# A gated linear recurrence fused with a feed-forward network: copies of v as a maximum, one exponential for the decays of a unit, copies shared out anew

## The chip, the cores and the metric

The kernel runs on one core of a Trainium2 chip. The core has a matrix engine (TensorE, PE in the profile; PEld are its weight loads), a vector engine (VectorE, DVE), a scalar engine (ScalarE, ACT), a general engine (GpSimd, POOL) and a queue engine (SyncE, SP) that here only issues DMA transfers. Each engine takes its own instructions in order; they wait for each other by semaphores. TensorE writes to PSUM, eight banks of 128 x 512 floats; all else that is on the chip lies in SBUF. The metric is the device time of one execution in microseconds (us).

## The reference

The inputs q, k, v and f_logit have the shape (4 batches, 8 heads, 768 tokens, 48), the three weights are 384 x 1536, 384 x 1536 and 1536 x 384, all in float32.

```python
f = 1.0 / (1.0 + np.exp(-f_logit))
state = np.zeros((B, H, D, D), dtype=np.float32)
for t in range(S):
    state = f[:, :, t, :, None] * state + np.einsum('bhd,bhe->bhde', k[:, :, t], v[:, :, t])
    y[:, :, t] = np.einsum('bhd,bhde->bhe', q[:, :, t], state)
...
x = np.ascontiguousarray(attn_out.transpose(0, 2, 1, 3)).reshape(B * S, H * D)
gate = np.maximum(x @ w_gate, 0.0)
val = x @ w_val
return (gate * val @ w_out).astype(np.float32)
```

So a linear attention whose state decays, channel by channel, by a factor of the token; its output, 3072 tokens by 384 channels, goes through a feed-forward network with a ReLU gate.

## The kernel before

**Tiling.** Tokens are taken in windows of 128; two windows in a row of one batch are a unit, so there are 24 windows and 12 units. `seq` goes through the four batches before it takes the next two windows of each. Four windows (two units) are a group of 512 tokens for the feed-forward part: 6 groups.

**A unit, step by step.** f, k, q and v of the unit are loaded by four DMAs of 384 KB (`load`, L533), into four buffers each. The two tokens of a pair lie beside each other in a partition, so everything comes as an even and an odd half. ScalarE makes exp(-f) in place (L609) and log(1 + that) in bf16 (`bneg`, L611). TensorE forms the cumulative sums with triangular matrices (`cum`, L618 and L619), the even ones either by two more matmuls or, where `even` is DVE, on VectorE by a subtraction (L622). ScalarE takes the exponentials of the sums with both signs (L630, L633, L640), into PSUM (`kps`, `qps`) or into SBUF (`expo`). VectorE or GpSimd multiplies them with q and k to `hats` (L652, L658). In units 0 to 5 TensorE transposes these (L692) and ScalarE or VectorE copies the result to `qkT` (L470, L471); in later units a DMA transposes (L714). TensorE forms the scores (L728); they are masked to `ptm`, by VectorE straight from PSUM (L741), or by a ScalarE copy (L736) and a GpSimd multiplication (L738). v is copied in bf16 to `vpad`, four half copies a unit, and in units 0 to 5 two more to `vrest` (`copy_on`, L470 and L471). The decays of a unit's two windows come from the totals of `bneg`: eight small matmuls against `halves` (`total`, L750) give them for both halves of the partitions, and ScalarE takes two exponentials of 64 partitions x 8 (L757), which leave the entries off the diagonal blocks of `dec` at the zeros it was filled with. The state's new part comes from TensorE (`state`, L767 or L777), the sum with the old state from VectorE (L584, or L579 for a first window), the multiplication by the decay from GpSimd (L587). The window's output comes from scores and state, transposed as the feed-forward part wants it (`intra`, L809, for windows in `pe_x`; ScalarE copies it to `xT`, L829) or in natural form (`natural`, L816 and L820; copy L834 to `xn`, and a DMA transposition, L836).

**The feed-forward part.** For each group and each of 12 blocks j of hidden columns: three matmuls for the gate and three for the value (L854), a ReLU on ScalarE (L860), the gated product on VectorE (L864) to `gT`. The first four j of group 0 are done in two halves of 256 tokens. Then 12 matmuls for each window's output (L880), a copy to `osb` on ScalarE (L895) and a store (L902). The outputs of a group are spread among the hidden products of the next one.

**What sets the order.** All operations are listed with their reads, writes, an assumed length, a latency and a priority (`Plan.add`). `Plan.schedule` goes through an assumed time and gives each engine the operation that could start first, by priority where several could; PSUM banks are given out in that run under a limit for each use (four for the feed-forward part). The order so found is written out engine by engine with the semaphore waits it needs. `chain` keeps operations of a sort in line. `first` is the order of the first loads, with what each waits for behind an @; a load also waits for the one six before it. The weights are loaded in four parts each on GpSimd's queue (L549). A table `on` names, for each unit, the engine of each step that has a choice: v00 to v11 and r0, r1 for copies of v, m00 to m11 for masks (POOL means ScalarE and GpSimd), q and k products, tq and tk for transposed copies; `q_lined` are the later units whose q products are made by token half, as the k products are. Until the planned time 24 matmuls on zeros (L939) are put ahead of TensorE's waits, as many as the planned gap takes.

Of the kernel before, what the change touches and what calls it, by code (L numbers as in the profile page):

```python
# [352 lines left out]
def bass_hgrn2_outer__then__ffn_reglu_kernel(  # L353
# [19 lines left out]
    GC = 4  # L373
# [51 lines left out]
    halves = sb("halves", [128, 2], BF16)  # L425
# [7 lines left out]
    pl.EASY = 30  # L433
# [34 lines left out]
    def copy_on(e, out, src):  # L468
        if e == "ACT":
            return sc.activation(out, src, AF.Copy)  # L470
        return engine[e].tensor_copy(out, src)  # L471

# [3 lines left out]
    def copy_t(e, n):  # L476
        return dict(occ=0.52, lat=0.16) if e == "ACT" else dict(occ=0.36, lat=0.13) if e == "DVE" else dict(occ=0.55, lat=0.1)
# [26 lines left out]
    for i in range(NA):  # L504
        fill("DVE", f"dec{i}", dec_all[:, i], 0.0, 8, -14)
# [21 lines left out]
    def load(n, u, after=()):  # L527
# [4 lines left out]
        behind = list(after) + (sent[-6:][:1] if len(sent) >= 6 else [])  # L532
# [39 lines left out]
    def new_state(kv, u, y, P):  # L572
# [4 lines left out]
        dk = [f"dec{ai}", f"dec{ai}_0", f"dec{ai}_1"]  # L577
# [12 lines left out]
    blocks = [(p, i) for p in range(NP) for i in range(3)]  # L590

    def unit(u):
# [11 lines left out]
        on.update({0: {'kps': True, 'qps': True, 'q0': 'POOL', 'q1': 'DVE', 'even': 'PE', 'm00': 'DVE', 'm01': 'DVE', 'm10': 'DVE', 'tk': 'DVE', 'm11': 'DVE', 'r1': 'ACT', 'tq': 'ACT', 'v11': 'ACT', 'v10': 'DVE', 'r0': 'DVE', 'v01': 'DVE', 'v00': 'POOL'}, 1: {'kps': True, 'r0': 'ACT', 'm01': 'DVE', 'm00': 'DVE', 'tq': 'ACT', 'v11': 'POOL', 'even': 'PE', 'tk': 'ACT', 'q1': 'DVE', 'v00': 'ACT', 'm11': 'POOL', 'r1': 'ACT', 'm10': 'DVE', 'v01': 'ACT', 'v10': 'POOL', 'q0': 'POOL', 'qps': False}, 2: {'tk': 'DVE', 'v01': 'POOL', 'kps': False, 'r1': 'ACT', 'r0': 'ACT', 'even': 'PE', 'q0': 'POOL', 'v00': 'ACT', 'v10': 'ACT', 'm00': 'DVE', 'v11': 'DVE', 'm01': 'DVE', 'm11': 'DVE', 'tq': 'DVE', 'q1': 'DVE', 'm10': 'POOL', 'qps': True}, 4: {'v10': 'ACT', 'v01': 'ACT', 'm00': 'DVE', 'q11': 'DVE', 'q00': 'POOL', 'q01': 'POOL', 'q0': 'POOL', 'kps': False, 'even': 'DVE', 'm01': 'DVE', 'v00': 'DVE', 'm10': 'POOL', 'q10': 'POOL', 'q1': 'DVE', 'm11': 'POOL', 'v11': 'DVE', 'qps': True, 'tq': 'DVE', 'r0': 'POOL', 'tk': 'DVE', 'r1': 'POOL'}, 10: {'m00': 'POOL', 'm10': 'POOL', 'q0': 'POOL', 'kps': False, 'q10': 'DVE', 'm01': 'POOL', 'q11': 'DVE', 'q00': 'POOL', 'v11': 'ACT', 'even': 'DVE', 'v01': 'DVE', 'v00': 'POOL', 'q01': 'POOL', 'q1': 'POOL', 'm11': 'DVE', 'v10': 'DVE'}, 9: {'v11': 'DVE', 'v10': 'ACT', 'even': 'DVE', 'kps': False, 'q1': 'DVE', 'm10': 'DVE', 'v00': 'ACT', 'm11': 'POOL', 'q11': 'DVE', 'm00': 'DVE', 'q00': 'DVE', 'q10': 'POOL', 'q0': 'POOL', 'q01': 'DVE'}, 3: {'kps': True, 'm00': 'POOL', 'm11': 'DVE', 'v11': 'ACT', 'm10': 'POOL', 'tk': 'ACT', 'v01': 'DVE', 'r1': 'ACT', 'tq': 'ACT', 'q1': 'POOL', 'v00': 'DVE', 'v10': 'ACT', 'q0': 'DVE', 'r0': 'POOL', 'm01': 'DVE', 'even': 'DVE', 'qps': False}, 5: {'q1': 'DVE', 'm00': 'DVE', 'kps': False, 'q11': 'POOL', 'v10': 'ACT', 'v00': 'ACT', 'even': 'DVE', 'q01': 'DVE', 'm11': 'POOL', 'q00': 'DVE', 'q0': 'POOL', 'v11': 'POOL', 'm01': 'DVE', 'q10': 'DVE', 'v01': 'DVE', 'm10': 'DVE', 'tq': 'DVE', 'r0': 'POOL', 'tk': 'ACT', 'r1': 'ACT', 'qps': False}, 11: {'q0': 'POOL', 'v01': 'ACT', 'q10': 'DVE', 'm00': 'POOL', 'q01': 'POOL', 'm11': 'POOL', 'q1': 'DVE', 'q00': 'DVE', 'kps': True, 'v11': 'ACT', 'm01': 'DVE', 'q11': 'DVE', 'even': 'PE', 'v00': 'ACT', 'm10': 'POOL', 'v10': 'POOL'}, 7: {'v10': 'POOL', 'kps': False, 'q1': 'POOL', 'v01': 'ACT', 'q11': 'POOL', 'm00': 'DVE', 'v11': 'DVE', 'even': 'PE', 'm10': 'POOL', 'm11': 'DVE', 'm01': 'DVE', 'q10': 'POOL', 'qps': False, 'q01': 'POOL'}, 8: {'m10': 'DVE', 'v11': 'ACT', 'q01': 'DVE', 'm01': 'POOL', 'even': 'DVE', 'q0': 'POOL', 'v10': 'ACT', 'q1': 'DVE', 'm00': 'DVE', 'kps': False, 'q11': 'DVE', 'q00': 'DVE', 'qps': False}, 6: {'v10': 'POOL', 'v01': 'DVE', 'q10': 'DVE', 'm10': 'DVE', 'kps': False, 'q1': 'POOL', 'even': 'PE', 'q01': 'DVE', 'm00': 'POOL', 'm01': 'POOL', 'q11': 'DVE', 'q00': 'POOL', 'm11': 'DVE', 'qps': True}}.get(u, {}))  # L604
# [64 lines left out]
        for y in range(2):  # L669
            vi = vis[y]  # L670
            for i in range(2):
# [75 lines left out]
        def total():  # L747
            for p in range(NP):
                for i in range(2):
                    mm = te.matmul(tot.ap[:, 2 * p:2 * p + 2], bn[:, i, 2 * p:2 * p + 2, :].rearrange("p h d -> p (h d)"),  # L750
                                   halves[:, :], start=(i == 0), stop=(i == 1), skip_group_check=True)
            return mm
        add("PE", total, ["halves"] + bkeys, [tot], occ=0.18, lat=PE_L, prio=P + 2, opens=[tot])
        for j in range(2):
            lo = 64 * j
            a0 = 2 * u % NA
            add("ACT", lambda lo=lo, j=j: sc.activation(  # L757
                dec_all[lo:lo + 64, a0:a0 + 2, :, j].rearrange("p b n -> p n b"),
# [148 lines left out]
    for g in range(NW // GC):  # L907
        for x in range(GC // 2):
# [3 lines left out]
            for op in pl.ops[before:]:  # L912
                op.slack = 2.5 if op.flow is not None else 0
# [112 lines left out]
```

## Time and profile before

| | us |
|---|---|
| median of 3 runs | 198.11 (197.93 to 198.9) |
| the profiled execution | 197.88 |
| its span, first to last instruction | 195.8 |
| TensorE busy | 187.1 (96%) |
| ScalarE busy | 137.9 (70%) |
| VectorE busy | 125.7 (64%) |
| GpSimd busy | 66.7 (34%) |

An engine's busy time is the time in which one of its instructions runs; matmuls overlap in the pipeline, so that the start of the next tells more of a matmul's cost than its own length. A group of instructions is named by line, engine, operation, output and inputs; behind the bar stand its busy time, the mean ns of one, and the idle time ahead of them with what ended it. The chain is followed back from the last instruction, at each step to what released it.

### The profile page before, as it was taken

What the parts mean: (1) busy time and instruction counts of PE and PEld (TensorE: products, weight loads), DVE (VectorE), ACT (ScalarE), POOL (GpSimd) and SP (SyncE); (2) the same over time, 40 slices, a digit from 0 to 9 for tenths busy, and PEclk for the clock granted to TensorE, in tenths of its full rate; (3) what the DMA queues carried; (4) which work ended last, traced back from release to release, by engine and by line L of the source; (5) the groups of instructions that cost most, each with busy time, mean ns of one, the idle gap of its engine ahead of it and who ended that gap; (6) DMA issues with size and microseconds to landing.
All of it is one profiled execution on the core that took longest, in us unless ns stands there. A gap on an engine that the chain in (4) does not pass through costs nothing.

```text
span 195.8 us, 4628 instructions
## 1 busy us (share of the span) xinstructions
PE 187.1 (96%) x1829; PEld 104.1 (53%) x1855; DVE 125.7 (64%) x227; ACT 137.9 (70%) x277; POOL 66.7 (34%) x94
## 2 busy tenths in 40 slices
PE   7899899998999999999999999999999999999995
PEld 2366585454565465555655455555555455544564
DVE  4576768948299899798997894975834423442300
ACT  4999857897699999999997775747643743344322
POOL 5179325516305835274606411603620600000000
DMA  5999999999999779999999107134544100111113
GB/s 159 324 323 198 203 254 239 203 258 257 255 301 295 211 193 308 222 236 298 161 214 173 66 20 142 44 75 112 31 106 94 44 32 8 44 40 40 40 40 121
DMA packets 74037, 31.25 MB, mean 160 GB/s; under 512 B 66209, under 2 KB 74017, under 8 KB 74017
## 3 DMA queue, kind: packets, MB, share of 16 engines
q1 hardware_dynamic: 69216, 27.43, 57.5%
q0 software_dynamic: 4800, 3.54, 11.9%
q8 instruction: 14, 0.23, 0.5%
q14 instruction: 7, 0.05, 0.1%
HBM read 25.95 MB, written 4.72 MB: 157 GB/s over the span
## 4 chain that ended last, share of the span: by engine, by line
PE 79%; ACT 14%; DVE 3%; DMA 2%; issue 1%
PE ps L854 44%; PE ps L880 22%; PE ps L809 3%; ACT qkT L470 2%; PE ps L728 2%; DMA f_in<-in_f_logit_dram 2%; ACT relu L860 2%; PE ps L692 1%; DVE ptm L741 1%; ACT vrest L470 1%; DVE vpad L471 1%; ACT vpad L470 1%; ACT ps L640 1%; ACT bneg L611 1%; ACT f_in L609 1%
## 5 line engine op out<-in xcount | busy, mean ns | idle before, releaser
L864 DVE TENSOR_TENSOR gT<-relu,ps 128x512 bf16<-128x512 bf16 (+1 forms) x76 | 49.6, 657 | 40.3 <-PE ps L854 33.7
L854 PE MATMUL ps<-xT,wv 128*128 128x512 bf16 (+1 forms) x221 | 57.8, 368 | 0.8 <-issue 0.5
L860 ACT ACTIVATE relu<-ps 128x512 bf16<-128x512 f32 (+1 forms) x76 | 43.6, 575 | 20.8 <-PE ps L854 20.4
L854 PE MATMUL ps<-xT,wg 128*128 128x512 bf16 (+1 forms) x212 | 55.6, 367 | 1.2 <-issue 0.3
L880 PE MATMUL ps<-wo,gT 128*128 128x384 bf16 (+2 forms) x300 | 52.0, 320 | 0.0
L880 PEld LDWEIGHTS ps<-wo,gT 128*128 128x128 bf16 x300 | 27.7, 98 | 19.1
L854 PEld LDWEIGHTS ps<-xT,wv 128*128 128x128 bf16 x228 | 21.1, 97 | 22.0
L854 PEld LDWEIGHTS ps<-xT,wg 128*128 128x128 bf16 x228 | 20.8, 97 | 18.9
L738 POOL TENSOR_TENSOR ptm<-ptm,seen 128x512 bf16<-128x512 bf16 x18 | 20.5, 1153 | 27.6 <-ACT ptm L736 27.5
L895 ACT ACTIVATE osb<-ps 128x384 f32<-128x384 f32 (+2 forms) x25 | 11.9, 481 | 21.7 <-PE ps L880 21.7
L587 POOL TENSOR_TENSOR st<-ssum,dec 128x384 bf16<-128x384 f32 x16 | 13.5, 846 | 27.7 <-DVE ssum L584 26.8
L741 DVE TENSOR_TENSOR ptm<-ps,seen 128x512 bf16<-128x512 f32 x30 | 19.0, 683 | 1.9 <-PE ps L728 1.6
L658 DVE TENSOR_TENSOR hats<-k_in,expo 64x384 bf16<-64x384 f32 x20 | 14.1, 706 | 0.3
L829 ACT ACTIVATE xT<-ps 128x384 bf16<-128x384 f32 x17 | 10.3, 605 | 3.7 <-PE ps L809 3.5
L736 ACT ACTIVATE ptm<-ps 128x512 bf16<-128x512 f32 x18 | 10.2, 601 | 3.6 <-PE ps L728 3.6
L470 ACT ACTIVATE vpad<-v_in 64x384 bf16<-64x384 f32 x23 | 12.0, 520 | 0.4
L658 POOL TENSOR_TENSOR hats<-q_in,expo 64x384 bf16<-64x384 f32 x7 | 7.2, 1022 | 12.6 <-ACT expo L633 12.3
L609 ACT ACTIVATE f_in<-f_in 128x768 f32<-128x768 f32 x12 | 10.1, 842 | 1.1 <-DMA f_in<-in_f_logit_dram 1.0
L939 PE MATMUL ps<-zeros 128*128 128x512 bf16 x35 | 9.8, 423 | 1.1 <-ACT dec L757 0.9
L611 ACT ACTIVATE bneg<-f_in 128x768 bf16<-128x768 f32 x12 | 10.0, 837 | 0.2
L471 POOL CAST vpad<-v_in 64x384 bf16<-64x384 f32 x12 | 6.4, 533 | 10.0 <-DMA v_in<-in_v_dram 6.5
L584 DVE TENSOR_TENSOR ssum<-ps,st 128x384 f32<-128x384 f32 x16 | 8.8, 551 | 1.1 <-PE ps L767 1.0
(79 smaller groups left out, 195.3 us busy)
## 6 DMA issues: line engine op xcount, KB each, us to landing
f_in<-in_f_logit_dram SPq DMA_DIRECT2D x12, 384.0 KB, 4.9
v_in<-in_v_dram SPq DMA_DIRECT2D x12, 384.0 KB, 5.2
q_in<-in_q_dram SPq DMA_DIRECT2D x12, 384.0 KB, 4.9
k_in<-in_k_dram SPq DMA_DIRECT2D x12, 384.0 KB, 4.9
out_dram<-osb SPq DMA_DIRECT2D x16, 192.0 KB, 2.7
out_dram<-osb SPq DMA_DIRECT2D x14, 96.0 KB, 2.2
wg<-in_moe_w_gate_dram POOLq DMA_DIRECT2D x4, 288.0 KB, 6.4
wv<-in_moe_w_val_dram POOLq DMA_DIRECT2D x4, 288.0 KB, 7.6
```

Source lines behind the costliest of these rows:

```text
L470: return sc.activation(out, src, AF.Copy)
L587: add(e, lambda: engine[e].tensor_tensor(t4(s_new), t4(tmp), rate, ALU.mult), [key] + dk, [f"S{b}_{y}"], prio=P + 2, **(dict(occ=0.79, lat ...
L609: add("ACT", lambda cut=cut: sc.activation(raw["f"][:, cut], raw["f"][:, cut], AF.Exp, scale=-1.0), [f"f{li}"], [f"f{li}"], prio=P, **act_ ...
L611: add("ACT", lambda: sc.activation(bn[:, :, :, 0:D], by_i["f"], AF.Ln, bias=1.0), [f"f{li}", f"bneg{bi}"], [f"bn{bi}"], prio=P, **act_t(2 ...
L658: op = add(e, lambda i=i, n=n, x=x, e=e, y=y, lo=lo, exps=exps: engine[e].tensor_tensor(hats[64 * i:64 * i + 64, hi, y, x, :, 0:D], by_i[n ...
L738: add("POOL", lambda pt=pt, mask=mask: gp.tensor_tensor(pt, pt, mask, ALU.mult), [f"raw{mis[y]}_{j}", "seen"], [f"raw{mis[y]}_{j}", f"ptm{ ...
L741: add("DVE", lambda pt=pt, mask=mask, s=sj[j]: ve.tensor_tensor(pt, s.ap[:, :].rearrange("p (n t) -> p n t", n=NP), mask, ALU.mult), [sj[j ...
L854: mm = te.matmul(bank.ap[:, 0:n], wt[:, kt, j * 128:(j + 1) * 128], xT[xi][:, kt, n0:n1], start=(kt == 0), stop=(kt == NK - 1))
L860: add("ACT", lambda: sc.activation(relu[ri][:, 0:n], gate.ap[:, 0:n], AF.Relu), [gate], [f"relu{ri}"], prio=P, **act_t(n))
L864: add("DVE", lambda: ve.tensor_tensor(gT[gi][:, j, n0:n1], relu[ri][:, 0:n], val.ap[:, 0:n], ALU.mult), [val, f"relu{ri}"], [f"gT{gi}_{j}_ ...
L880: mm = te.matmul(bank.ap[:, 0:cut[1] - cut[0]], gT[gi][:, j, r * C:(r + 1) * C], wo[:, j, cut[0]:cut[1]], start=(j == 0), stop=(j == NJ - 1))
L895: add("ACT", lambda bank=bank, oi=oi, cut=cut, wide=wide: sc.activation(osb[oi][:, cut[0]:cut[1]], bank.ap[:, 0:wide], AF.Copy), [bank], [ ...
```

## The change

- A copy of v can go to a third place, `DVE1`: VectorE takes a maximum over an added axis of length one (`tensor_reduce`) in place of a copy. 15 of the 60 half copies of v (`vpad` and `vrest`) are of this form; plain VectorE copies fall from 14 to 3.
- `halves` gets a second half of columns, and a 16-column matmul ahead of the totals (`other` against `away`) adds 8 x 2 x 16 = 256 wherever the entry is to be zero, so that one exponential of 128 partitions x 16 gives all decays of a unit and `dec` is no longer filled.
- Copies of outputs (`o0`, `o1`) and of x (`x0`, `x1`) have an engine by unit: 15 of 25 output copies and 7 of 24 x copies stand on VectorE.
- In every unit the k exponential now stays in PSUM (`kps` true), where VectorE's product reads it; the q products that VectorE made from `expo` in SBUF move to GpSimd or to factors in PSUM (`qps`).
- The order: another `first`; five loads in flight instead of six; a lower priority of the feed-forward part on TensorE (60 for 20); a smaller margin on DMA landings in the plan (1 for 2.5, from the planned time 34 for 30); five j of group 0 in halves instead of four; `pace` holds the cumulative sums of units 4 to 11 behind given products; other `pe_x` and `q_lined`. `longer` is empty, since `0 - size` is never positive.

The lines, cut; of the table `on` the entries that differ are given by unit as before>after:

```diff
-    first = 'f0 f1 v0 q0 k0 v1 f2 wg0@f2 wg2@f0 wv0@k0 wg1@f2 wv1@f0 wv3@f0 k1 q1 k2 wv2@k2 q2@wv1 wg3@q2 wo0@f0 wo2@f1 wo1@f1 wo3@k0 f3 k3@wv2 q3 v2 v3@wo2'.split()
+    first = 'f0 v0 f1 k0 q0 f2 wg2@f2 wg0@f2 wv0@f0 wv1@v0 k1 wg1@k1 q1 wv2@q1 v1 k2@wv0 q2 wg3@q2 wv3@v0 wo1@f0 wo0@f1 wo2@f0 wo3@f0 f3@wg2 q3@wv0 k3@wg1 v2@wo1 v3@wv0'.split()
-    pe_x = {0, 1, 2, 3, 4, 5, 6, 7, 8, 10, 11, 14, 15, 16, 17, 22, 23}
-    q_lined = {0, 1, 3, 4, 5, 6, 7, 9, 10}
+    pe_x = {0, 1, 2, 3, 4, 5, 6, 7, 9, 10, 11, 12, 13, 21, 22, 23}
+    q_lined = {0, 1, 4, 7, 8, 9, 10}
...
-    pl.EASY = 30
+    pl.EASY = 34
...
     def copy_on(e, out, src):
+        if e == "DVE1":
+            return ve.tensor_reduce(out, src.unsqueeze(len(src.shape)), mybir.AxisListType.X, ALU.max)
...
     def copy_t(e, n):
+        if e == "DVE1":
+            return dict(occ=0.47, lat=0.13)
...
-        behind = list(after) + (sent[-6:][:1] if len(sent) >= 6 else [])
+        behind = list(after) + (sent[-5:][:1] if len(sent) >= 5 else [])
...
         def total():
+            te.matmul(tot.ap[:, 0:4 * NP], other[:, :], away[:].rearrange("p n b j -> p (n b j)"), start=True, stop=False,
+                      skip_group_check=True)
             for p in range(NP):
                 for i in range(2):
-                    mm = te.matmul(tot.ap[:, 2 * p:2 * p + 2], bn[:, i, 2 * p:2 * p + 2, :].rearrange("p h d -> p (h d)"),
-                                   halves[:, :], start=(i == 0), stop=(i == 1), skip_group_check=True)
+                    mm = te.matmul(tot.ap[:, 4 * p:4 * p + 4], bn[:, i, 2 * p:2 * p + 2, :].rearrange("p h d -> p (h d)"),
+                                   halves[:].rearrange("p b j -> p (b j)"), start=False, stop=(i == 1), skip_group_check=True)
...
-        for j in range(2):
-            lo = 64 * j
-            a0 = 2 * u % NA
-            add("ACT", lambda lo=lo, j=j: sc.activation(
-                dec_all[lo:lo + 64, a0:a0 + 2, :, j].rearrange("p b n -> p n b"),
-                tot.ap[lo:lo + 64, 0:2 * NP].rearrange("p (n b) -> p n b", n=NP), AF.Exp, scale=-1.0),
...
+        add("ACT", lambda: sc.activation(dec_all[:, a0:a0 + 2, :, :].rearrange("p b n j -> p n b j"),
+                                         tot.ap[:, 0:4 * NP].rearrange("p (n b j) -> p n b j", n=NP, b=2), AF.Exp, scale=-1.0),
+            [tot], [f"dec{a0}", f"dec{a0 + 1}"], prio=P + 3, occ=0.2, lat=0.12)
...
-            add("ACT", lambda: sc.activation(lined, bank.ap[:, 0:HD].rearrange("q (n i t) -> q n i t", n=NK, i=2), AF.Copy),
+            add(e, lambda: copy_on(e, lined, bank.ap[:, 0:HD].rearrange("q (n i t) -> q n i t", n=NK, i=2)),
                 [bank], x_key, prio=P + 8, occ=0.48, lat=0.16)
...
-              prio=P + 20, opens=[gate])
+              prio=P + 60, opens=[gate])
...
-                add("ACT", lambda bank=bank, oi=oi, cut=cut, wide=wide: sc.activation(osb[oi][:, cut[0]:cut[1]], bank.ap[:, 0:wide], AF.Copy),
-                    [bank], [f"osb{oi}_{n}"], prio=P, **act_t(wide))
+                add(e, lambda bank=bank, oi=oi, cut=cut, wide=wide, e=e: copy_on(e, osb[oi][:, cut[0]:cut[1]], bank.ap[:, 0:wide]),
+                    [bank], [f"osb{oi}_{n}"], prio=P, **(act_t(wide) if e == "ACT" else dve_t(wide)))
...
-                op.slack = 2.5 if op.flow is not None else 0
-        for r0, r1, js in {0: [(0, 2, range(0, 4)), (2, 4, range(0, 4)), (0, 4, range(4, 12))]}.get(g, [(0, GC, range(NJ))]):
+                op.slack = 1 if op.flow is not None else 0
+        for r0, r1, js in {0: [(0, 2, range(0, 5)), (2, 4, range(0, 5)), (0, 4, range(5, 12))]}.get(g, [(0, GC, range(NJ))]):
...
+    pace = {4: 0, 6: 22, 9: 29, 8: 32, 10: 46, 5: 6, 7: 18, 11: 44}
+    for u, n in pace.items():
+        firsts[u].follows.append(inner[n])
```

```text
unit 0: m01 DVE>POOL, q1 DVE>POOL, r0 DVE>POOL, v00 POOL>DVE, v01 DVE>POOL, v10 DVE>DVE1, v11 ACT>DVE, x0 o0 o1 ACT>DVE
unit 1: m10 DVE>POOL, m11 POOL>DVE, qps False>True, r1 ACT>DVE1, tk ACT>DVE, v11 POOL>DVE, x0 o0 o1 ACT>DVE
unit 2: even PE>DVE, kps False>True, qps True>False, q1 DVE>POOL, r1 ACT>DVE1, tk tq DVE>ACT, v11 DVE>DVE1, x0 x1 o0 o1 ACT>DVE
unit 3: even DVE>PE, m01 m11 DVE>POOL, qps False>True, tk ACT>DVE, v00 DVE>DVE1, v01 DVE>POOL, x0 o0 o1 ACT>DVE
unit 4: kps False>True, v00 DVE>DVE1, v11 DVE>POOL, x0 o0 o1 ACT>DVE
unit 5: even DVE>PE, kps False>True, m00 DVE>POOL, m11 POOL>DVE, q1 DVE>POOL, r0 POOL>DVE1, r1 ACT>POOL, v01 DVE>ACT, v11 POOL>DVE1
unit 6: kps False>True, m10 DVE>POOL, v01 DVE>DVE1, v10 POOL>DVE1, o0 o1 ACT>DVE
unit 7: even PE>DVE, kps False>True, v11 DVE>DVE1, x1 o1 ACT>DVE
unit 8: kps False>True, q00 q01 q11 DVE>POOL, o0 ACT>DVE
unit 9: kps False>True, q00 q01 q11 DVE>POOL, v00 ACT>DVE1, v10 ACT>POOL, v11 DVE>DVE1
unit 10: kps False>True, qps False>True, m10 POOL>DVE, v01 v10 DVE>DVE1, o0 ACT>DVE
unit 11: even PE>DVE, m10 POOL>DVE, q00 q10 q11 DVE>POOL, v00 v11 ACT>POOL
```

More of the change, by code (lines that the diff above doesn't have):

```diff
@@ L424, in bass_hgrn2_outer__then__ffn_reglu_kernel @@
     below = sb("below", [128, C], BF16)
-    halves = sb("halves", [128, 2], BF16)
+    halves = sb("halves", [128, 2, 2], BF16)
+    other = sb("other", [128, 128], BF16)
+    away = sb("away", [128, NP, 2, 2], BF16)
     seen = sb("seen", [128, C], BF16)
@@ L836, in out_of @@
+            add(e, lambda: copy_on(e, xn[ni][:, :], bank.ap[:, 0:HD]), [bank], [f"xn{ni}"], prio=P + 8,
+                **(act_t(HD) if e == "ACT" else dve_t(HD)))
             op = add("SP", lambda: sy.dma_start(dst, xn[ni][:, :], transpose=True),
@@ L954, in bass_hgrn2_outer__then__ffn_reglu_kernel @@
     stores = [op for op in order["SP"] if op.writes and op.writes[0].startswith("out")]
+    size = len(order["DVE"]) + sum(max(0, len(waits[op]) - 1) for op in order["DVE"])
+    longer = set(order["DVE"][-80:][:max(0, 0 - size)])
+    spare = sb("spare", [128, 1], BF16)
     def run(name, eng):
```

43 lines of the change are left out of this document (26 added, 17 removed).

## The prediction

> **What bounds the kernel now.** I read the page first, then busy time by stage, the chain that ended last, TensorE's instructions in time, and the duration groups.
>
> ```profile
> span 195.8 us, 4628 instructions
> ...
> PE 79%; ACT 14%; DVE 3%; DMA 2%; issue 1%
> ```
>
> The chain's shares put TensorE first; the 14% on ScalarE lie almost wholly in the front. By stage (start and end, length; then busy us and instructions of TensorE, its weight loads, VectorE, ScalarE, GpSimd; granted clock, DMA share, GB/s):
>
> ```profile
> 6.04:21.85 15.81, 14.17 (x204) 8.61 (x208) 11.54 (x22) 15.55 (x34) 10.48 (x14) 1.00 1.23 268
> 21.85:54.20 32.35, 31.42 (x387) 19.19 (x390) 21.82 (x40) 24.68 (x50) 12.77 (x16) 1.00 1.11 242
> 54.20:185.60 131.40, 129.65 (x1169) 69.64 (x1188) 89.61 (x147) 92.17 (x186) 40.81 (x45) 1.00 0.57 131
> ```
>
> The clock is granted in full. In the first of these stages ScalarE is busy 15.55 of 15.81 us, and TensorE's 14.17 contain matmuls on zeros that compute nothing. From 21.85 on TensorE hardly rests. The chain in order of time (start, us, what), and TensorE's own instructions around the points that matter:
>
> ```profile
> 0.81 3.44 DMA f_in<-in_f_logit_dram
> 4.26 0.85 ACT f_in L609
> ...
> 21.16 0.19 ACT dec L757
> ...
> 51.07 0.51 PE ps L809 x28
> ...
> 66.46 0.17 PE ps L816 x4
> 66.63 0.20 PE ps L820 x8
> ...
> 69.71 0.45 PE ps L777 x16
> ...
> 71.56 0.55 PE ps L728 x16
> ...
> 165.51 3.88 PE ps L854 x18
> ...
> 181.07 1.95 PE ps L880 x12
> ```
>
> ```profile
> 6.70 0.34 PE L750 MATMUL ps<-halves,bneg 128*128 128x2 bf16 x8
> 6.90 3.18 PE L939 MATMUL ps<-zeros 128*128 128x512 bf16 x14
> ...
> 18.99 0.49 PE L854 MATMUL ps<-xT,wg 128*128 128x256 bf16 x3
> ...
> 21.85 0.49 PE L854 MATMUL ps<-xT,wv 128*128 128x256 bf16 x3
> 22.18 0.49 PE L854 MATMUL ps<-xT,wg 128*128 128x256 bf16 x3
> 22.51 0.49 PE L854 MATMUL ps<-xT,wv 128*128 128x256 bf16 x3
> ...
> 23.27 0.50 PE L854 MATMUL ps<-xT,wg 128*128 128x256 bf16 x3
> ...
> 48.54 0.41 PE L809 MATMUL ps<-ptm,vpad 128*32 128x128 bf16 x16 [0.57 <-DVE vpad L471]
> ```
>
> From 4.26 to 21.35 the chain is ScalarE's queue. After it, one matmul of 512 columns costs 3.88/18 = 0.216 us, one of 384 columns 1.95/12 = 0.163, three of 256 columns 22.18 - 21.85 = 0.33, and the one stop of size is 0.57 us at 48 us (idle time and its releaser in brackets). So the time is the front up to steady hidden products, plus a fixed amount of matmul, plus stops. The change can win at most what the front wastes and that stop; it loses wherever it lets TensorE wait later.
>
> **The change part by part.** Prices, from the groups (out of the last part of each line: busy us, mean ns) and single rows:
>
> ```profile
> L609 ACT ACTIVATE f_in<-f_in 128x768 f32<-128x768 f32 x12 | 10.1, 842 | 1.1 <-DMA f_in<-in_f_logit_dram 1.0
> L630 ACT ACTIVATE ps<-ps 128x384 f32<-128x384 f32 x8 | 3.7, 478 | 0.0
> L470 ACT ACTIVATE qkT<-ps 128x1024 bf16<-128x1024 bf16 x6 | 5.9, 1017 | 0.0
> L757 ACT ACTIVATE dec<-ps 64x8 f32<-64x8 f32 x24 | 4.3, 180 | 0.9 <-PE ps L750 0.6
> L829 ACT ACTIVATE xT<-ps 128x384 bf16<-128x384 f32 x17 | 10.3, 605 | 3.7 <-PE ps L809 3.5
> L652 DVE TENSOR_TENSOR hats<-q_in,ps 128x384 bf16<-128x384 f32 x6 | 3.1, 546 | 0.3 <-DMA q_in<-in_q_dram 0.3
> L658 DVE TENSOR_TENSOR hats<-k_in,expo 64x384 bf16<-64x384 f32 x20 | 14.1, 706 | 0.3
> L584 DVE TENSOR_TENSOR ssum<-ps,st 128x384 f32<-128x384 f32 x16 | 8.8, 551 | 1.1 <-PE ps L767 1.0
> L741 DVE TENSOR_TENSOR ptm<-ps,seen 128x512 bf16<-128x512 f32 x30 | 19.0, 683 | 1.9 <-PE ps L728 1.6
> ```
>
> ```profile
> 10.91 0.69 DVE L471 COPY qkT<-ps 128x1024 bf16<-128x1024 bf16 x1 [0.71 <-PE ps L692]
> ...
> 13.07 2.48 DVE L741 TENSOR_TENSOR ptm<-ps,seen 128x512 bf16<-128x512 f32 x4
> ```
>
> Four masks in a run take 2.48, so 0.62 each against a mean of 0.683: in a run I take some 0.06 off, and as much on ScalarE.
>
> *Matmul work.* The built order has 12 more matmuls, the 16-column one ahead of each unit's totals; eight small ones take 6.90 - 6.70 = 0.20, so 12 x 0.025 = +0.3. The even sums go from TensorE to VectorE in units 2, 7 and 11 and the other way in 3 and 5: one pair of 384 columns fewer, -0.33. One window fewer is made transposed: 0.51 becomes 0.17 + 0.20, -0.14. Five column blocks of group 0 in halves instead of four: six matmuls at 0.11 for three at 0.216, nothing. Together -0.2, on the path. Zero matmuls fall from 39 to 34; they fill waits and count for nothing.
>
> *Loads.* f1 is issued third, not second. Loads start some 1.2 us apart (rows below), so it lands at 4.25 + 2 x 1.2 = 6.7, where ScalarE, held till 6.6 by unit 0's sums in either order, takes it behind one exponential: no cost. Five loads in flight instead of six, and k2 behind wv0, let the weights meet fewer loads; I count no gain, since products could begin at 18.99 as it was. wg3 waits for q2 on GpSimd's queue, with wv3, four wo parts and unit 2's q products behind it; by the place of their users they have until about 35 us.
>
> ```profile
> 1.93 1.06 SPq L533 DMA_DIRECT2D v_in<-in_v_dram  x1
> 3.03 1.19 SPq L533 DMA_DIRECT2D q_in<-in_q_dram  x1
> ```
>
> *The front, walked in the new order.* ScalarE from 6.62: q exponential 0.4, f1's exponential 0.75, k 0.4, one decay 0.15, q 0.4, f1's logarithm 0.75 (as long as L609), last k 0.45: 9.9. VectorE has the last k product of unit 0 at 10.75 (0.55, behind a q product). Transposes 0.71 and their copy 0.69: 12.1. From here VectorE's queue rules: product 0.5, state 0.5, product 0.5, sum 0.45, three masks 1.86, two products 0.95, one v copy 0.45, the next transposed copy 0.65, the x copy 0.5, one v copy 0.35: 6.7, so 18.8. Then TensorE's state 0.45 and scores 0.55, and the first hidden product goes at 19.85. ScalarE, rid of copies, waits for unit 1's transposes at 16.7; its half of x (1.0 and 0.55 after 17.85) is there at 19.4, its first ReLU starts at 21.4, behind five instructions, and frees the bank of the fourth product at 21.85. From there: product, product, window 3 (0.5), three products at 0.33. Eight products are done at 24.05. In the rows above, five are (18.99, 21.85, 22.18, 22.51, 23.27). Three more, 3 x 0.33 = **-1.0 us**. The front's bottleneck passes from ScalarE to VectorE, which is why emptying ScalarE brings one microsecond and not seven.
>
> *Copies as a maximum.* A plain copy on VectorE could be caught behind GpSimd; the 0.57 us stop is such a case (the tile's row gives minimum/median/maximum ns):
>
> ```profile
> L471 DVE CAST vpad<-v_in x13: 342/357/1678, 6.7 to 107.6; 64x384 bf16<-64x384 f32 x13
> ```
>
> ```profile
> 45.43 1.15 POOL L738 TENSOR_TENSOR ptm<-ptm,seen 128x512 bf16<-128x512 bf16 x1 [1.12 <-ACT ptm L736]
> ```
>
> No row shows the maximum. Bounds: 0.36, the free copy, and 0.55, L584 with as many elements and a second operand; I take 0.47, between them and nearer L584's kind. 15 of them then cost VectorE 15 x 0.11 = 1.6 us over free copies, and no long ones remain. The k products now read their factor from PSUM: 20 x (0.706 - 0.55) = 3 us less. The stop at 48 us goes for this and because the states of units 2 and 3 now stand behind 33 output matmuls (33 x 0.163 = 5.4 us), late v or not: **-0.6**.
>
> The Trainium skill's VectorE: DVE Perf Modes speaks against this edit: its perf-mode tier table gives tensor_reduce one element a cycle only, and its rules for kernel authors call it the slowest VectorE op, where an fp32 copy in SBUF takes two; from its 2293 and 1227 ns for 2048 elements I estimate 384 x 0.52 ns = 0.2 us more a copy, 3 us in all. By that figure the sum below would be 0.2 us longer. No row here shows it yet.
>
> *Output and x copies on VectorE.* 15 output and 7 x copies leave ScalarE, which was not late after 22 us: worth nothing by itself. They cost VectorE 22 x 0.5 = 11 us (between a free 0.36 and L741's 0.62), and the place where that counts is the turn from group 0 to group 1:
>
> ```profile
> 40.00:60.00 20.00, 19.14 (x251) 10.82 (x253) 12.89 (x23) 17.14 (x34) 5.44 (x7) 1.00 1.01 274
> ```
>
> VectorE had 12.9 of 20 us there. In the new order, from unit 2's new state to the copies of unit 4's transposes, it has 2 states, 2 sums, 1 subtraction (0.56 each), 3 x copies (0.5), 2 output copies (0.46), 4 products (0.51), 1 maximum, 2 gated products (as masks, 0.66), 2 transposed copies: 19 instructions, 10.4 us. TensorE's own work up to the scores of unit 4 is 15 output matmuls 2.45, four windows 1.6, two states 0.9, sums 0.55, seven hidden products 4.5, transposes 0.9: 10.9. Slack 0.5, and what lies beyond it stops TensorE. Bounds 0 and 3 us (0.18 each, as far as 0.36 is from L584); I take **+0.4**, 0.05 each less the slack.
>
> *Decays, pacing, tail.* One 16-column exponential for two of 8 frees 12 x 0.18 on ScalarE, off the path. The order edges hold units 4 to 11 behind products, but their x still comes some 6 us ahead of the group that reads it. The last output products and copies are as before: 0.
>
> Sum: 195.8 - 0.2 - 1.0 - 0.6 + 0.4 = 194.4. The profiled execution took 197.88, 2.1 more than its span, and stands 0.2 under the median of 198.11: 194.4 + 2.1 + 0.2 = 196.7, rounded up to **196.8** for the walk's own roughness.
>
> **Rivals.** *VectorE becomes the bound at the turn (slower).* For it: 10.4 of 10.9 us, with like crowding at the next group. Against it: four banks let products run ahead. It decides from 0.15 us more an instruction: 19 x 0.15 - 0.5 = 2.4, and 1.0 at the next turn: 196.8 - 0.4 + 3.4 = 199.8.
> *The front does not shorten.* VectorE idles nowhere from 12 to 19 us in the walk, so one late v1 or wv0 gives the 1.0 back: 197.8. DMA at a share of 1.23 in that stage speaks for it; that wv0's first user comes at 20.2, against it.
> *It shortens more.* If the v copies cost 0.36 and ScalarE's first ReLU does not queue behind five instructions, up to 1.5 us more: 195.3.
>
> **How the numbers follow.** 0.5%, one microsecond, is about what a measurement can tell from no change. The forecast holds 0.50 (own range 195.7 to 198.0; 0.36 of it under 197.1, 0.14 above), the shorter front 0.13 (faster), no front gain 0.17 (0.02 faster, 0.13 same, 0.02 slower), VectorE as the bound 0.20 (slower). Faster 0.51, same 0.27, slower 0.22. The range 194.6 to 200.0 leaves a tenth on each side.
>
> **What would show it.** Right: eight products by 24 us; no stop on vpad near 48; TENSOR_REDUCE near 470 ns with none above 600. Wrong: TensorE waiting on VectorE (x, transposed copies, state) between 45 and 60 us, or its first product after 21 us. The forecast fails if VectorE's new copies cost over 0.6 us each, or if q2 lands after 30 us and holds wg3.

## The result

The changed kernel takes 196.06 us (median of 4 runs, 195.99 to 196.28); the kernel before, run beside it, 198.44 (197.93 to 198.9). The ratio is 0.988 (95% interval 0.985 to 0.991): 1.2% faster, where 196.8 had been predicted. The page of the changed kernel, its profiled execution at 196.28 us:

```profile
span 194.5 us, 4615 instructions
...
PE 187.0 (96%) x1827; PEld 104.7 (54%) x1850; DVE 131.1 (67%) x247; ACT 123.2 (63%) x239; POOL 75.2 (39%) x105
...
PE 73%; ACT 11%; DVE 10%; issue 3%; DMA 2%; POOL 0%; SPq 0%; DVEq 0%
```

The last line is the chain: ScalarE's share has fallen from 14% to 11%, VectorE's has risen from 3% to 10%. Busy time by stage (start and end, length, then TensorE's busy us and instructions), first of the kernel before, then of the changed one:

```profile
24.00:60.00 36.00, 35.01 (x401) 20.79 (x394) 25.72 (x47) 28.66 (x58) 12.25 (x15) 1.00 1.09 253
60.00:100.00 40.00, 39.23 (x405) 21.96 (x411) 35.83 (x60) 38.85 (x81) 21.50 (x25) 1.00 0.98 239
100.00:125.00 25.00, 24.58 (x285) 13.31 (x289) 19.71 (x33) 17.94 (x37) 7.80 (x9) 1.00 0.54 100
125.00:200.00 75.00, 67.94 (x491) 36.50 (x496) 28.98 (x46) 31.87 (x63) 11.51 (x11) 1.00 0.25 57
```

```profile
24.00:60.00 36.00, 35.79 (x410) 22.23 (x412) 27.24 (x53) 27.57 (x54) 18.11 (x23) 1.00 1.04 244
60.00:100.00 40.00, 39.37 (x463) 21.73 (x468) 33.53 (x59) 34.36 (x68) 21.39 (x26) 1.00 1.04 261
100.00:125.00 25.00, 24.24 (x215) 13.63 (x217) 19.37 (x34) 13.97 (x31) 14.57 (x17) 1.00 0.44 93
125.00:200.00 75.00, 66.65 (x475) 35.47 (x479) 33.12 (x54) 28.92 (x55) 8.14 (x8) 0.98 0.21 53
```

TensorE's busy time left after 24 us falls from 166.76 (the four rows added) to 166.05 us, 0.71 less, because more is done ahead of it: without the matmuls on zeros TensorE is busy there for 10.89 us instead of 10.11 (20.95 - 10.06, 20.34 - 10.23), and in the whole span for 176.9 us in both kernels. Its idle time, length less busy, goes from 0.99 to 0.21 us between 24 and 60, from 0.77 to 0.63 up to 100, and from 0.42 **up** to 0.76 between 100 and 125. Behind 125 us nothing changes (with the spans' ends, 2.86 and 2.85; the clock of 0.98 in the last row falls behind TensorE's last matmul, and up to 194 us it is 1.00). Together -0.71 - 0.78 - 0.14 + 0.34 = -1.29, the 1.3 us between the two spans.

Two of these numbers vary from trace to trace. The profiled execution is the slowest of the four, and in traces of kernels with the same front (below) the first hidden product starts up to 0.27 us earlier. The 0.34 us contain a stop near 117 us that is 0.17 to 0.56 us long in the traces that leave this stretch as it is.

In the front, the changed kernel's instructions (start, us, engine, line; idle time and its releaser in brackets):

```profile
11.55 0.69 DVE L475 COPY qkT<-ps 128x1024 bf16<-128x1024 bf16 x1 [0.79 <-PE ps L703]
...
18.12 1.02 ACT L474 ACTIVATE qkT<-ps 128x1024 bf16<-128x1024 bf16 x1 [1.41 <-PE ps L703]
...
18.78 0.36 DVE L475 CAST vpad<-v_in 64x384 bf16<-64x384 f32 x1
...
19.19 0.21 PE L787 MATMUL ps<-vpad,hats 64*128 64x96 bf16 x1 [0.61 <-ACT qkT L474]
...
20.38 0.50 PE L866 MATMUL ps<-xT,wg 128*128 128x256 bf16 x3 [0.22 <-DVE st L589]
...
24.17 0.49 PE L866 MATMUL ps<-xT,wv 128*128 128x256 bf16 x3
```

ScalarE now waits 1.41 us for the transposes, and the state's matmuls at 19.19 start when two things end together, at 19.14: ScalarE's transposed copy (18.12 + 1.02) and VectorE's last copy of v (18.78 + 0.36). The product (of a hidden block, three matmuls) at 24.17 is the eighth; five were started by 24 us before, seven are now.

The stop on `vpad` at 48 us is gone. Two others have come, near 110 and 117 us; the weight load tells the first wait plainly:

```profile
104.56 7.43 SPq L725 DMA_TRANSPOSE qkT<-hats  x3
...
110.72 0.20 PEld L777 LDWEIGHTS ps<-vpad,hats 128*128 128x128 bf16 x4 [0.30 <-DVE hats L669]
...
112.03 1.52 SPq L917 DMA_DIRECT2D out_dram<-osb  x2
113.61 1.32 SPq L725 DMA_TRANSPOSE qkT<-hats  x1
...
116.94 0.62 PE L739 MATMUL ps<-qkT 48*128 48x128 bf16 x16 [0.42 <-DMA qkT<-hats]
```

### The profile page after: what moved, and what is told of

Its sections match the earlier page's. It is cut to its first block, busy times and chain, and to the rows that moved or that the text cites. A ratio compares the mean times of both kernels' runs of the same rounds, so it can differ in the third digit from the quotient of the medians.

```text
span 194.5 us, 4615 instructions
## 1 busy us (share of the span) xinstructions
PE 187.0 (96%) x1827; PEld 104.7 (54%) x1850; DVE 131.1 (67%) x247; ACT 123.2 (63%) x239; POOL 75.2 (39%) x105
## 4 chain that ended last, share of the span: by engine, by line
PE 73%; ACT 11%; DVE 10%; issue 3%; DMA 2%; POOL 0%; SPq 0%; DVEq 0%
PE ps L866 37%; PE ps L894 21%; PE ps L819 3%; PE ps L958 3%; DVE ptm L752 2%; PE ps L703 2%; ACT relu L872 2%; PE ps L739 2%; DVE hats L669 2%; DVE gT L878 2%; DMA qkT<-hats 2%; ACT ptm L747 1%; ACT expo L644 1%; ACT f_in L620 1%; ACT ps L651 1%
## 5 line engine op out<-in xcount | busy, mean ns | idle before, releaser
L749 POOL TENSOR_TENSOR ptm<-ptm,seen 128x512 bf16<-128x512 bf16 x20 | 22.8, 1154 | 23.1 <-ACT ptm L747 23.1
L752 DVE TENSOR_TENSOR ptm<-ps,seen 128x512 bf16<-128x512 f32 x28 | 17.8, 683 | 2.4 <-PE ps L739 2.3
L474 ACT ACTIVATE osb<-ps 128x384 f32<-128x384 f32 (+2 forms) x10 | 4.6, 459 | 16.5 <-PE ps L894 16.5
L475 DVE COPY osb<-ps 128x384 f32<-128x384 f32 x15 | 8.3, 554 | 8.3 <-PE ps L894 8.2
L669 DVE TENSOR_TENSOR hats<-k_in,ps 64x384 bf16<-64x384 f32 x24 | 13.2, 550 | 0.6 <-ACT ps L651 0.3
L747 ACT ACTIVATE ptm<-ps 128x512 bf16<-128x512 f32 x20 | 11.1, 598 | 4.1 <-PE ps L739 4.0
L669 POOL TENSOR_TENSOR hats<-q_in,expo 64x384 bf16<-64x384 f32 x12 | 11.9, 995 | 1.3 <-ACT expo L644 0.6
L651 ACT ACTIVATE ps<-ps 128x384 f32<-128x384 f32 x24 | 10.8, 484 | 0.0
L474 ACT ACTIVATE xT<-ps 128x384 bf16<-128x384 f32 x11 | 6.6, 601 | 6.2 <-PE ps L819 5.9
L474 ACT ACTIVATE vpad<-v_in 64x384 bf16<-64x384 f32 x19 | 9.9, 520 | 0.3
```

What stands on the lines that cost most here:

```text
L651: add("ACT", lambda i=i, ex=ex: sc.activation(bc[i].ap[:, 0:HD] if in_place else ex[:, 1, :], bc[i].ap[:, 0:HD], AF.Exp, scale=1.0), [bc[i ...
L669: op = add(e, lambda i=i, n=n, x=x, e=e, y=y, lo=lo, exps=exps: engine[e].tensor_tensor(hats[64 * i:64 * i + 64, hi, y, x, :, 0:D], by_i[n ...
L747: add("ACT", lambda pt=pt, s=sj[j]: sc.activation(pt, s.ap[:, :].rearrange("p (n t) -> p n t", n=NP), AF.Copy), [sj[j]], [f"raw{mis[y]}_{j ...
L749: add("POOL", lambda pt=pt, mask=mask: gp.tensor_tensor(pt, pt, mask, ALU.mult), [f"raw{mis[y]}_{j}", "seen"], [f"raw{mis[y]}_{j}", f"ptm{ ...
L752: add("DVE", lambda pt=pt, mask=mask, s=sj[j]: ve.tensor_tensor(pt, s.ap[:, :].rearrange("p (n t) -> p n t", n=NP), mask, ALU.mult), [sj[j ...
```

## The experiments

The edits of the changed kernel leave the written order of every engine as it is, but for what they name; they ran beside the kernel before, and are compared with 196.06 us and, where a trace is used, by the start of the same matmul in both traces.

**The maximum.** In the changed kernel, the maxima as plain copies:

```diff
         if e == "DVE1":
-            return ve.tensor_reduce(out, src.unsqueeze(len(src.shape)), mybir.AxisListType.X, ALU.max)
+            return ve.tensor_copy(out, src)
```

> The changed kernel with its 15 VectorE copies of v emitted as plain copies again, the order of every engine kept. Theory one (the prediction's: a maximum costs 0.547 us against a free 0.36 but cannot be caught behind GpSimd): two to four of the 15 copies take over 0.6 us, one of them stops TensorE for 0.2 to 0.6 us, time 196.2 to 196.7. Theory two (the kind of copy does not matter, what removed the 0.57 us stop was the order): all 15 copies near 0.36 us, those between 12 and 19 us shorten the front by up to 0.2, time 195.8 to 196.0.

196.88 us (6 runs, 196.77 to 197.06), 0.8 slower than with the maximum. The copies by tile (count, then ns minimum/median/maximum), first of the changed kernel, then of this one, and what this one shows near 110 us:

```profile
L472 DVE TENSOR_REDUCE vpad<-v_in x12: 536/548/550, 5.9 to 106.5; 64x384 bf16<-64x384 f32 x12
```

```profile
L472 DVE CAST vpad<-v_in x12: 343/357/1450, 6.0 to 106.9; 64x384 bf16<-64x384 f32 x12
...
L472 DVE CAST vrest<-v_in x3: 505/1062/1330, 17.0 to 64.6; 64x384 bf16<-64x384 f32 x3
```

```profile
106.34 1.00 POOL L669 TENSOR_TENSOR hats<-q_in,expo 64x384 bf16<-64x384 f32 x1 [0.64 <-ACT expo L644]
...
106.89 1.45 DVE L472 CAST vpad<-v_in 64x384 bf16<-64x384 f32 x1
...
107.30 0.82 POOL L597 TENSOR_TENSOR st<-ssum,dec 128x384 bf16<-128x384 f32 x1
...
111.99 0.20 PEld L777 LDWEIGHTS ps<-vpad,hats 128*128 128x128 bf16 x4 [1.20 <-DVE hats L669]
111.99 0.34 PE L777 MATMUL ps<-vpad,hats 128*128 128x96 bf16 x4 [1.03 <-DVE hats L669]
```

Theory one holds in kind, with its price set too low: six of the 15 take over 0.6 us, and the mean of all 15, 0.64 us (the profile's 557 and 966 ns, weighted), is above the maximum's 0.547. TensorE falls back by 0.19 us near 66 us and by 1.1 us between 107 and 112 us, of which 0.48 come back because the stop near 117 us is gone. Most of the 1.1 us is the copy of 1.45 us, 0.9 longer than the maximum. It starts beside a GpSimd product, ends 0.22 us after the GpSimd multiplication that follows (107.30 + 0.82), and stands where VectorE has no slack, so the state's weight loads wait 1.20 us there instead of 0.30. All 15 maxima of the changed kernel lie between 536 and 550 ns.

One half of theory two holds as well. Between 24 and 60 us TensorE is idle for 0.21 us in this kernel too (busy 35.79 of 36.00), although a copy of 1.33 us stands at 42.0. So the new order alone is enough to remove the stop near 48 us, and what the maximum earns in it lies further on.

The Trainium skill's SBUF — State Buffer, section Who interferes with whom, says that on trn2 a VectorE copy can take the port pair that it shares with GpSimd, that the first to issue keeps the pair for its whole instruction while the other is fully blocked, and that tensor_reduce never contends. This pair of traces agrees; the copy of 1.45 us was held past two GpSimd instructions in a row. The rule that the prediction weighed, in the Trainium skill's VectorE: DVE Perf Modes, perf-mode tier table, was right in size (0.55 against 0.36 us, 0.2 estimated) and would have decided wrongly in this order: the dearer instruction is the one that can be planned.

The same on the kernel before, where VectorE's copies of v become maxima (an edit of `copy_on` alone; they are 14, not the 16 of the expectation):

```diff
-        return engine[e].tensor_copy(out, src)
+        return ve.tensor_reduce(out, src.unsqueeze(len(src.shape)), mybir.AxisListType.X, ALU.max) if e == "DVE" and src.dtype == F32 else engine[e].tensor_copy(out, src)
```

> The kernel before with its 16 VectorE copies of v emitted as a maximum, nothing else. Theory one (the stop at 48 us is the 1.68 us copy caught behind GpSimd): no maximum above 0.6 us, and the stop shrinks from 0.57 to 0.2 to 0.35, no further, since GpSimd's second mask ended at 48.27 only 0.27 before the window's start; time 0.2 to 0.4 less than before, and 0 to 0.2 more in the front where the copies are 0.19 dearer. Theory two (order alone): stop and time unchanged, within 0.2.

198.11 us against 198.81 (ratio 0.997, 0.995 to 0.999). But the median span is 195.9 us in both, so the 0.7 us lie outside of it. In the trace:

```profile
47.93 0.41 PE L809 MATMUL ps<-ptm,vpad 128*32 128x128 bf16 x16
...
73.41 0.35 PE L809 MATMUL ps<-qkT,st 128*32 128x128 bf16 x12 [0.19 <-DVE ptm L741]
```

The window that started at 48.54 starts at 47.93, with no wait, so the stop did hang on the caught copy. That is more than theory one had it: the GpSimd mask that it took for the next bound ends at 48.17, when the window has started, and so is none. But the matmuls that started at 73.62 start at 73.41, only 0.21 us earlier, and from 91.5 us on 0.02 us are left. Two maxima ahead of masks (at 70.91 and 90.17), 0.19 dearer each, stand where VectorE has nothing to spare; the first shows as the wait of 0.19 us for a mask. In this order the maximum gives back elsewhere what it wins.

**Copies of outputs and x.** The 20 that VectorE makes after 30 us, back on ScalarE (`now` holds the engine being written; `copy_on` takes ScalarE's form when that is ACT):

```diff
+    back = [o for o in order["DVE"] if str(o.writes[0])[:2] in ("os", "xT", "xn") and o.start > 30]
+    order["DVE"] = [o for o in order["DVE"] if o not in back]
+    order["ACT"] = sorted(order["ACT"] + back, key=lambda o: o.start)
...
```

> The changed kernel with the 20 output and x copies that VectorE makes after 30 us put back on ScalarE at the same places of the plan. Theory one (these copies keep VectorE without a gap from 101 to 113 us and cause the 0.29 us stop before the state at 110.7 and part of the 0.58 us stop before the scores at 116.9): both stops shrink, 0.3 to 0.6 us less, 195.5 to 195.8. Theory two (copies cost nothing on either engine): stops and time unchanged, 195.9 to 196.2. Theory three (ScalarE gets late with its ReLUs): new waits of TensorE on relu, 196.5 or more.

196.22 us (195.95 to 196.67), median span 194.3 as with the copies on VectorE: by time theory two holds. The weight loads at the first stop:

```profile
109.72 0.45 PEld L741 LDWEIGHTS ps<-qkT 48*128 48x128 bf16 x16 [0.42 <-issue]
...
110.27 0.20 PEld L779 LDWEIGHTS ps<-vpad,hats 128*128 128x128 bf16 x4
```

The state's weight loads wait 0.10 us here (110.17 to 110.27), and 0.30 or 0.31 in the other traces of the changed kernel, but for the one with plain copies of v. No copy stands in VectorE's last 4 us ahead of this place (a sum, a maximum, two gated products, four k products), but VectorE reaches the k products 0.4 us sooner against TensorE. So theory one is right about this stop: the copies cost 0.2 us of it, too little to show in the medians. The second stop is 0.23 us long and not 0.42, which says nothing, since it varies from 0.17 to 0.56 without the edit.

**The queue.** One transposing DMA ahead of the two stores:

```diff
+    op = [o for o in order["SP"] if o.writes[0].startswith("qkT")][7]
+    at = order["SP"].index(op)
+    order["SP"][at - 2:at + 1] = [op] + order["SP"][at - 2:at]
...
```

> The changed kernel with one transposing DMA on SyncE's queue (second half of unit 9's q and k) put ahead of the two output stores that stood before it. Theory one (the stop before the scores at 116.94 is the queue: the two stores take 1.52 us of it ahead of the transposition): the scores start 0.4 to 0.6 us earlier with no wait on a DMA, time 195.5 to 195.7. Theory two (the transposition waits for GpSimd's q products, or its 3.28 us to landing is set by other transfers): stop stays above 0.3, time 196.0 to 196.2.

195.7 us (195.56 to 195.94). SyncE's queue and the scores:

```profile
104.48 8.89 SPq L725 DMA_TRANSPOSE qkT<-hats  x4
...
113.42 1.22 SPq L917 DMA_DIRECT2D out_dram<-osb  x2
...
116.37 0.62 PE L739 MATMUL ps<-qkT 48*128 48x128 bf16 x16
```

The scores start at 116.37, not 116.94, with no wait on a DMA, and theory one holds. Of the 0.57 us this trace was 0.08 ahead before the stop, so the exchange won 0.5 us here; the medians differ by 0.36.

**What bounds the front.** Idle work of two instructions, once on VectorE, once on ScalarE, and on ScalarE in the kernel before; the first as an example:

```diff
+    mark = [o for o in order["DVE"] if str(o.writes[0]).startswith("raw")][2]
...
+            if op is mark:
+                for n in range(2):
+                    ve.tensor_reduce(idle[:, n], zeros[:].unsqueeze(2), mybir.AxisListType.X, ALU.max)
```

> The changed kernel with two idle maxima of 512 columns (about 0.6 us each) added on VectorE behind the third mask of unit 0, near 16.0 us. Theory one (VectorE sets the front): the first hidden product and everything behind it 0.9 to 1.2 us later, time 196.9 to 197.3. Theory two (VectorE has slack in the front): 0.4 us later or less, time 196.0 to 196.5.

> The changed kernel with two idle copies of 512 columns (about 0.6 us each) added on ScalarE behind its last copy of v of unit 1, near 16.6 us. Theory one (ScalarE waits 1.41 us there and is not the bound of the front): nothing moves, time 195.9 to 196.2. Theory two (ScalarE is still the bound, or shares it): the first hidden product 0.5 to 1.1 us later, time 196.5 to 197.2.

> The kernel before with the same two idle copies on ScalarE behind its last copy of v of unit 1, near 15.3 us. Theory one (ScalarE is the bound of the front before the change): the products that began at 21.85 begin 0.9 to 1.2 us later, and the time is 0.9 to 1.2 us above that of the kernel before. Theory two (it is not): 0.3 us or less.

The idle work and what follows it, in these three kernels:

```profile
16.00 1.27 DVE L1000 TENSOR_REDUCE idle<-zeros 128x512 bf16<-128x512 bf16 x2
...
17.79 0.62 PE L703 MATMUL ps<-ident,hats 128*128 128x128 bf16 x8 [1.24 <-DVE hats L663]
...
21.60 0.50 PE L866 MATMUL ps<-xT,wg 128*128 128x256 bf16 x3 [0.22 <-DVE st L589]
```

```profile
16.36 1.13 ACT L1000 ACTIVATE idle<-zeros 128x512 bf16<-128x512 bf16 x2
...
17.94 1.02 ACT L474 ACTIVATE qkT<-ps 128x1024 bf16<-128x1024 bf16 x1 [0.37 <-PE ps L703]
...
20.20 0.50 PE L866 MATMUL ps<-xT,wg 128*128 128x256 bf16 x3 [0.22 <-DVE st L589]
```

```profile
15.39 1.15 ACT L977 ACTIVATE idle<-zeros 128x512 bf16<-128x512 bf16 x2
...
22.88 0.49 PE L854 MATMUL ps<-xT,wv 128*128 128x256 bf16 x3
```

On VectorE 1.27 us move the first hidden product from 20.38 to 21.60 and the time to 197.41 (197.0 to 197.83). On ScalarE 1.13 us do not delay it (20.20; this trace was 0.18 ahead before them, and ScalarE's wait shrinks from 1.41 to 0.37), and the time is 196.28 (196.19 to 196.51). Before the change they moved the products of 21.85 to 22.88, 1.03 us; the median span grew from 195.9 to 197.0, the time only by 0.4% (0.1 to 0.7), and the profiled execution lost 0.8 us more at 41 us to a load of v that landed late. So theory one's account holds three times, and the bound of the front has passed from ScalarE to VectorE. The times lie just beyond its ranges: 197.41 for up to 197.3, 196.28 for up to 196.2, and before the change 0.4% for 0.9 to 1.2 us, though the span grew by 1.1.

Does VectorE's relief then pay? Two copies of v go to ScalarE's wait:

```diff
+    dec = [o for o in order["ACT"] if str(o.writes[0]).startswith("dec")][2]
+    back = [o for o in order["DVE"] if o.writes[0] in ("vrest1_1", "v_3_1")][:2]
+    for n, o in enumerate(back):
+        o.start = dec.start + 0.001 * (n + 1)
...
```

> The changed kernel with two of unit 1's copies of v (a maximum of 0.55 us at 17.0 and a plain copy of 0.36 us at 18.8) moved from VectorE to ScalarE, into the 1.41 us that ScalarE waits from 16.7 us. Theory one (the prediction's: VectorE's queue sets the front from 12 to 19 us, ScalarE waits): VectorE's queue is 0.9 us shorter, the first hidden product starts 0.3 to 0.9 us before 20.38, time 195.2 to 195.8 against 196.06. Theory two (ScalarE's transposed copy from 18.12 to 19.14 and TensorE's transposes set it): the first hidden product stays within 0.1 of 20.38, time 195.9 to 196.2.

```profile
18.20 1.02 ACT L477 ACTIVATE qkT<-ps 128x1024 bf16<-128x1024 bf16 x1 [0.45 <-PE ps L706]
...
20.10 0.50 PE L869 MATMUL ps<-xT,wg 128*128 128x256 bf16 x3
...
22.04 0.50 PE L869 MATMUL ps<-xT,wv 128*128 128x256 bf16 x3 [0.18 <-ACT relu L875]
```

Of 0.9 us taken from VectorE 0.28 arrive at the first hidden product, and a wait on a ReLU follows: the product of 22.23 starts at 22.04, 0.19 earlier. This trace was 0.1 us behind up to the copies (18.20 for 18.12), so they won 0.4 us at the first product and 0.3 behind it. ScalarE's transposed copy, which ends at 19.22, is next. Both theories are right in part, and 196.03 us (195.59 to 196.32) is no measurable gain by itself.

**The turn.** The same idle work on VectorE behind the first x copy of the turn:

```diff
+    mark = [o for o in order["DVE"] if str(o.writes[0]).startswith("xT")][2]
...
```

> The changed kernel with two idle maxima (1.27 us together, as measured in the front) added on VectorE behind its first x copy of the turn from group 0 to group 1, at 48.5 us. Theory one (the prediction's: 0.5 us of slack in this stretch): TensorE 0.6 to 0.9 us later from 50 us on, time 196.7 to 197.0. Theory two (the stretch had more slack, since the trace shows VectorE idle for 0.45 us at 49.4 and 0.56 us at 52.4): 0.3 us later or less, time 196.0 to 196.4.

196.14 us (195.97 to 196.56). TensorE is 0.15 us later from 51.0 us on, as the trace of this kernel shows:

```profile
48.44 1.26 DVE L1000 TENSOR_REDUCE idle<-zeros 128x512 bf16<-128x512 bf16 x2
...
51.15 0.35 PE L819 MATMUL ps<-qkT,st 128*32 128x128 bf16 x12
```

That window started at 51.00. So VectorE had 1.1 us of slack behind this place, not 0.5: theory two.

**The time around the span.** The medians differ by 2.4 us, the spans only by 1.6: in 53 runs of the kernel before, beside these experiments, 195.9 is the median span, and 2.05 to 3.66 us lie around it; in the changed kernel 194.3, with 1.69 to 1.78. Two programs were lengthened with one-column instructions:

```diff
...
+            for n in range(2 if op in marks else 0):
+                sc.activation(idle[:, 2 * marks.index(op) + n:][:, 0:1], zeros[:, 0:1], AF.Copy)
```

> The changed kernel with 46 one-column copies added on ScalarE behind its last 23 ReLUs, so that ScalarE has as many instructions as before the change. The question is the time around the span, 1.7 to 1.8 us in the changed kernel and 2.05 to 3.6 us before. Theory one (the length of ScalarE's program sets it; 20 more ScalarE instructions gave 1.85 to 2.0): 2.05 us or more around the span. Theory two (it does not): 1.7 to 1.8. The span is not expected to grow by more than 0.2 us.

> The kernel before with 30 one-column fills added on VectorE behind its last 15 gated products, so that VectorE has as many instructions as after the change. Theory one (the length of VectorE's program sets the time around the span): 1.7 to 1.9 us around the span in every run, time near 197.7. Theory two (it does not): 2.05 to 3.6 us as before, time 198.4 to 199.0.

The changed kernel with ScalarE's program longer than before the change (285 instructions to 277) has 1.70 to 1.73 us around the span (196.02 in all). The kernel before with VectorE's program longer than after it (257 to 247) has 1.70 to 2.96 (198.26), under 2 us in three of ten runs. The first length is ruled out; the second explains at most a part. What sets this time stays open.

**Both edits.** The swap and the two moved copies:

> The changed kernel with both edits that shortened TensorE's waits: the transposing DMA ahead of the two stores, and the two copies of v of unit 1 on ScalarE. Theory one (the two gains lie in different stages and add): 0.57 us from the one and 0.2 to 0.4 us from the other, span 193.4 to 193.8, time 195.2 to 195.5. Theory two (what the front gains is lost again to a later wait): time 195.6 to 195.8, as with the swap alone.

195.49 us (195.39 to 195.55), ratio to before 0.986 (0.983 to 0.988): 0.57 us below the changed kernel, 0.2 below the swap alone.

```profile
span 193.7 us, 4617 instructions
...
19.89 0.50 PE L869 MATMUL ps<-xT,wg 128*128 128x256 bf16 x3
```

Theory one, at the upper end of its range: the gains add. By the medians the exchange alone won 0.36 us and the moved copies alone 0.03, so 0.57 together contain some scatter; in the traces the copies win 0.3 us behind the first hidden product with and without the exchange.

## Why the prediction was right, and where not

- *Sign and span.* 194.4 us was the sum, 194.5 the profiled span, 194.3 the median one. That they meet so closely is partly luck: front and matmul work gave 0.5 us less than forecast, the stop and the stretch behind it 0.3 more, and the 0.4 us charged to the turn were lost elsewhere. The forecast time of 196.8 is 0.7 too long because the 2.1 us around the span became 1.75, and because 0.2 for the median and a rounding up of 0.1 were put on top.
- *Front and matmul work, -1.0 and -0.2.* Measured 0.71 together. As far as busy time tells, all of it is the front's (10.89 us of work ahead of 24 us for 10.11), and the 0.2 us of matmul work do not show (176.9 us in both). In the front the mechanism was right (idle work on VectorE costs what it lasts, on ScalarE nothing). Mis-sized was the walk's "VectorE's queue to 18.8": the queue ended at 19.14, with a maximum at 0.55 and an x copy at 0.58 in place of 0.45 and 0.5; and the product waited another 0.22 us for a bank that the new state's product on VectorE frees, a wait that the walk lacked. The walk had eight products done by 24.05; the eighth starts at 24.17, and at 23.97 in a faster trace with the same front (ScalarE's program lengthened), so this sign of being right was missed by a product.
- *The stop, -0.6.* Right: the idle time from 24 to 60 us fell by 0.78. Of the two reasons given either is enough by itself: the maximum in the order before leaves no wait at 47.93, and the new order with plain copies is idle for 0.21 us as with maxima.
- *The turn, +0.4.* Right in size, wrong in place and cause. Nothing waits at 45 to 60 us, and VectorE had 1.1 us of slack there. The 0.34 us came back between 100 and 125 us, at a transposition that stands behind two stores on SyncE's queue; the exchange shows that the queue's order makes this stop. Where it comes from is argued only, since no run takes it back: the table of edits lists, and the sum left out, that units 8 and 9 moved q products to GpSimd, after which their DMA transpositions reach that queue late. For a moved step each queue behind it should have been walked.
- *The maximum, 0.47.* It takes 0.547, at the upper bound: what was nearer was the two-operand row (0.551). None is above 0.55.
- *Output and x copies, worth nothing.* Right by the medians (moved back: 196.22), though 0.2 us of the stop near 110 us are theirs, and each takes 0.55 to 0.58 us and not 0.46 to 0.5.
- *Not separated.* No run takes back the k factors in PSUM, the one exponential for the decays, the order of the loads or `pace` by itself.
- *Rivals.* VectorE as the bound at the turn fell, but the mechanism is alive ahead of 110 us, where the state's weight loads wait 0.30 us for VectorE, and 1.20 with plain copies. "The front does not shorten" fell. "It shortens more" (195.3) rested on copies of 0.36, which did not come; the measured time lies as far above it as below the forecast.

## What to carry to other kernels

On a full engine choose the instruction whose time is certain over the one that is shorter at its best: a copy that always takes 0.55 us beat one that takes 0.36 or, beside GpSimd, up to 1.45, by 0.8 us. In an order not made for it, it left the span as it was. When a step moves to another engine, follow its result to every queue that takes it up; here a transposition behind two stores stopped TensorE for 0.42 us, and exchanging them won 0.36. Idle work added to an engine shows whether it is the bound, but not what relief brings: 1.27 us more cost 1.2, 0.9 us less won 0.3.

## What the runs showed of the hardware that had not been expected

- On VectorE an instruction over 384 columns of 4-byte data took 0.55 to 0.58 us in nearly every form: maximum of 64 partitions in SBUF 0.547, copy of 128 partitions out of PSUM 0.554, product with a factor in PSUM 0.550. The plain copy within SBUF is faster (0.357 where nothing held it up).
- The copy is not the only form that is held up beside GpSimd. Products of two operands in SBUF were too, in the kernel before (first row), and those with the factor in PSUM, in the changed one (second row), were not; so the change took a second kind of uncertain instruction off VectorE. The seven of the 20 that took over 0.6 us each overlap a GpSimd instruction:

```profile
L658 DVE TENSOR_TENSOR hats<-k_in,expo x20: 544/555/1371, 76.9 to 130.7; 64x384 bf16<-64x384 f32 x20
```

```profile
L669 DVE TENSOR_TENSOR hats<-k_in,ps x24: 534/552/558, 78.0 to 148.2; 64x384 bf16<-64x384 f32 x24
```

- The time around the span differs by kernel (1.69 to 1.78 against 2.05 to 3.66 us) and is a third of the gain; with the 20 copies back on ScalarE it was 1.84 to 2.01. No run here shows its cause.
